# Loading q of the first three attention steps as pairs of tokens in a fused attention and mixture-of-experts kernel

## Chip, cores and metric

One core of one Trainium2 chip runs the whole program. The metric is the device time of one execution, in microseconds (us), as the median of several runs; less is better.

## What is computed

Two blocks follow one another. The first is a lightning attention over q, k and v of shape (4, 8, 768, 64) (batch, heads, tokens, head size), with one decay rate per head. The second is a top-1 mixture of eight experts over the 3072 rows of width 512 that the attention gives. Cut to what matters:

```python
for b in range(S // 64):                     # lightning attention, all of it per batch and head
    intra = (qb @ kb.T * Dmask) @ vb
    inter = (qb * lam_pow) @ kv_state
    out[b] = intra + inter
    kv_state = lam_block * kv_state + (kb * rev_pow).T @ vb
x = out.transpose(0, 2, 1, 3).reshape(3072, 512)
e = argmax(x @ w_gate)                       # one expert per row
y = softmax_max * relu(x @ w1[e]) @ w2[e]
```

## The kernel before

The attention runs in 12 steps of 128 tokens for two batches (`steps`, line 90): step 0 is batches 0 and 1, step 1 batches 2 and 3, both of the first 128 tokens; step 2 is batches 0 and 1 of the next 128 tokens, and so on. A step's q, k and v are one load of 512 KB each (line 117), with a token in a partition and the 16 head rows of 256 bytes beside one another: 2048 packets of 256 bytes. Only step 0 loads its q and k in four parts each (line 115; per half of the heads and per batch, 128 KB). All of these loads are issued by SyncE in the order written, the first nine ahead of the program (lines 124 to 130), later ones by `begin` four steps ahead; they go into three tiles of their own (`q_in`, `k_in`, `v_in`) and two that later hold weights (`room`).

In each step TensorE turns q and k to (head size, tokens): eight products with the identity each into PSUM (`turned`, line 242; `tq` and `tk`), two heads at a time. For each half `s` of the heads, ScalarE copies `tq` to `qT` and `tk` to `kT` (lines 252 and 264). In step 1 alone (`m.n == 0 and m.b > 0`, line 249) VectorE copies `tq` instead. From step 2 on VectorE also multiplies `tq` by `qdec` into `qs_room` (line 256), the query that meets the running state. GpSimd makes `kd` = k times `kdec` (line 270).

Then come, in the order in which TensorE has them: `score` (line 280, `sp`, 32 products; VectorE multiplies by the decay mask into `mt`, line 287, four instructions), the state's part (line 309, from step 2 on), `grow` (line 348, `cp`), `attend` (line 322, `op`), the copy of `op` into `xT` by ScalarE (lines 334 and 340; in step 0 half of the second by VectorE, line 1197), and the gate's products (`lgT`, line 374) and the turn back to rows (`tx`, line 383) in `leave`. TensorE's order is fixed by `pin`, so it waits for whatever its next product needs.

VectorE makes the decay tables once, by scans along tokens: `decay` (line 178, eight scans) and `kdec` (line 183), and then `later_decays` (lines 1010 to 1018): two copies to `lam_pair`, four scans to `qdec`, one copy to `sdec`. Their place is set by `with tc.issue_after(keys_made.ins): later_decays()` (line 1175), right after `kdec`.

After the attention the rows are gathered by expert through lists in memory, and each expert's two products run with weights of 2 MB each.

Of the kernel before, what the change touches and what calls it, by code (L numbers as in the profile page):

```python
# [10 lines left out]
F32 = mybir.dt.float32  # L11
# [12 lines left out]
def kernel(  # L24
# [34 lines left out]
    P = 128  # L59
# [37 lines left out]
    for j, name in enumerate("qkv"):  # L97
        own = [qkv.tile([P, 2, H, D], F32, tag=name, name=f"{name}_in") for i in range(3)]
        homes[name] = own + [
            room[:, j].rearrange("p (b h d) -> p b h d", b=2, h=H) for room in w_room]  # L100

    def load(i, names, first=False):

        if i >= len(steps) or (i, names[0]) in loaded:
            return
        n, b0 = steps[i]
        parts = (slice(0, H // 2), slice(H // 2, H)) if first else (slice(0, H),)
        for name in names:
            loaded[i, name] = homes[name][i % len(homes[name])]
        for hs, name in itertools.product(parts, names):  # L110
            src = {"q": q, "k": k, "v": v}[name][b0:b0 + 2, hs, n * C:(n + 1) * C, :]
            to = loaded[i, name]
            if first:
                for b in range(2):
                    nc.sync.dma_start(out=to[:, b, hs], in_=src[b].rearrange("h s d -> s h d"))
            else:
                nc.sync.dma_start(out=to.rearrange("p b h d -> p (b h) d"),
                                  in_=src.rearrange("b h s d -> s (b h) d"))
# [113 lines left out]
    def pin(inst):  # L232
        tc.keep_in_program_order(inst)
        return inst
# [4 lines left out]
    def turned(src, s, t):  # L239
# [2 lines left out]
            pin(nc.tensor.transpose(t[:, i, b, :], src[:, b, h:h + 2, :], ident))  # L242
        return t

    def turn_q(m, s):
        shp = turned_shape
        tq = turned(m.q, s, bank(2 * s, shp, "tq"))
        qT = work.tile(shp, F32, tag="qT", name="qT")
        if m.n == 0 and m.b > 0:
            pin(nc.vector.tensor_copy(qT, tq))  # L250
        else:
            nc.scalar.copy(qT, tq)
        m.qT.append(qT)
        if m.n > 0:
            qsT = qs_room[:, next(qs_slots)]
            nc.vector.tensor_mul(  # L256
                qsT, tq, qdec[:, s * HP // 2:(s + 1) * HP // 2].unsqueeze(2).to_broadcast(shp))
            m.qsT.append(qsT)
# [913 lines left out]
                mybir.DependencyClass.Sync, mybir.DependencyReason.DATA),  # L1172
                reason="the gathers have the DMA engines first")

    with tc.issue_after(keys_made.ins):
        later_decays()
    idle = bank(5, [P, P], "idle")
    for i in range(10):
        pin(nc.tensor.matmul(idle, lhsT=zeros, rhs=zeros, start=True, stop=True))
# [18 lines left out]
    one = begin(1)  # L1198
    for s in range(2):
        turn_q(one, s)  # L1200
    leave(cur, between=lambda: [turn_k(one, s) for s in range(2)])()
    for s in range(2):
        score(one, s)
# [241 lines left out]
```

## Time and profile before

| | before |
|---|---|
| median of 3 runs | 432.18 us |
| the runs | 431.16, 432.18, 433.41 us |
| the profiled execution's own time | 429.92 us |
| its span, first to last instruction | 428.1 us |
| TensorE busy | 97% of the span |
| VectorE, ScalarE, GpSimd busy | 62%, 41%, 60% |
| TensorE's granted clock | full speed in all 40 slices |

The profile's span is 1.82 us shorter than the time of the same execution, and that execution 2.26 us shorter than the median. All starts below are in us from the start of the span. A chain of waits is followed back from the last instruction: each piece is what released the next. "Issue" pieces and queues such as SPq are time of a sequencer.

### The profile page before, as it was taken

The numbers are of one execution on the slowest core, as the hardware profiler recorded it, in microseconds if no ns is written. First come the engines' busy times: TensorE is split into PE (matmuls) and PEld (weight loads), VectorE is DVE, ScalarE is ACT, GpSimd is POOL, SyncE is SP. The second block draws the span as 40 slices with busy tenths as digits, with TensorE's granted clock in tenths as the row PEclk, the third lists the DMA queues.
The fourth block names the chain that finished last, engine by engine and source line by source line (L and its number), as shares of the span: only waits on it lengthen the run. The fifth ranks groups of instructions, "written<-read, shape, count | busy, mean of one in ns | idle before, by whom it ended". The sixth has DMA issues, their size and how long they took to land.

```text
span 428.1 us, 9730 instructions
## 1 busy us (share of the span) xinstructions
PE 416.5 (97%) x3775; PEld 392.9 (92%) x3776; DVE 265.0 (62%) x587; ACT 174.1 (41%) x319; POOL 255.9 (60%) x209
## 2 busy tenths in 40 slices
PE   8999999999999997999999999999999999999995
PEld 7889999988878986999999999999999999999964
DVE  6656657787566546765558757554775565556454
ACT  3365455565431434350544154345414525331131
POOL 4242657471353357777938856794875878559043
PEclk9999999999999999999999999999999999999999
DMA  9999999999876748968359947966974894652121
GB/s 174 208 240 246 249 240 230 230 233 237 239 257 189 239 63 248 297 190 316 57 123 195 346 81 155 318 183 117 268 276 81 186 380 94 157 200 47 29 78 64
DMA packets 164545, 83.06 MB, mean 194 GB/s; under 512 B 145923, under 2 KB 145959, under 8 KB 164496
## 3 DMA queue, kind: packets, MB, share of 16 engines
q1 hardware_dynamic: 155024, 63.21, 60.9%
q0 software_dynamic: 5536, 12.88, 10.2%
q10 hardware_dynamic: 3936, 6.31, 4.4%
q8 instruction: 31, 0.51, 0.5%
q14 instruction: 18, 0.15, 0.1%
HBM read 58.96 MB, written 12.72 MB: 167 GB/s over the span
## 4 chain that ended last, share of the span: by engine, by line
PE 80%; DVE 5%; DMA 5%; ACT 3%; SPq 2%; POOL 2%; issue 2%; POOLq 0%; ACTq 0%; DVEq 0%
PE p L734 30%; PE p L932 26%; PE sp L280 5%; PE op L322 4%; PE cp L348 2%; PE tk L242 2%; PE tx L383 2%; PE op L309 2%; PE tq L242 2%; PE p L780 2%; DMA xg<-xs,list_0a 1%; PE p L788 1%; DMA xg<-xs,list 1%; PE lgT L374 1%; SPq L583 1%
## 5 line engine op out<-in xcount | busy, mean ns | idle before, releaser
L539 POOL DMA_INDIRECT out_dram<-o_room,list x24 | 25.5, 1064 | 53.9 <-DMA decay<-planes_q 23.0
L745 ACT ACTIVATE hT<-hT 128x418 f32<-128x418 f32 (+6 forms) x56 | 28.1, 520 | 33.1 <-DVE hT L742 32.1
L734 PE MATMUL p<-xgT,w1t 128*128 128x209 f32 (+6 forms) x224 | 41.1, 326 | 0.0
L287 DVE TENSOR_TENSOR mt<-sp,decay 128x512 f32<-128x512 f32 x48 | 29.8, 682 | 14.5 <-PE sp L280 14.4
L734 PEld LDWEIGHTS p<-xgT,w1t 128*128 128x128 f32 x224 | 37.2, 189 | 0.4 <-issue 0.4
L624 ACT COPY u_qT<-p 128x418 f32<-128x418 f32 (+6 forms) x14 | 6.7, 479 | 68.2 <-PE p L734 68.2
L932 PE MATMUL p<-hT,w2t 128*128 128x209 f32 (+5 forms) x192 | 33.6, 328 | 0.0
L472 POOL DMA_INDIRECT slots<-entry,slot_i x24 | 23.8, 990 | 13.8 <-PE tl L397 6.0
L932 PEld LDWEIGHTS p<-hT,w2t 128*128 128x128 f32 x192 | 32.0, 189 | 0.0
L533 POOL DMA_INDIRECT xg<-xs,list x25 | 25.2, 1010 | 11.0 <-issue 6.1
L742 DVE TENSOR_TENSOR hT<-p,u_kd 128x418 f32<-128x418 f32 (+6 forms) x28 | 15.6, 559 | 20.3 <-PE p L734 20.3
L270 POOL TENSOR_TENSOR kd<-k_in,kdec 128x512 f32<-128x512 f32 x12 | 12.4, 1042 | 21.7 <-issue 10.3
L280 PE MATMUL sp<-qT,kT 64*128 64x128 f32 x384 | 24.7, 279 | 0.5 <-DVE qs_room L256 0.5
L661 POOL TENSOR_TENSOR s_q<-w1t 128x1024 f32<-128x1024 f32 x7 | 16.5, 2357 | 14.3 <-DVE t_xT L719 12.6
L280 PEld LDWEIGHTS sp<-qT,kT 64*128 64x128 f32 x384 | 22.5, 188 | 2.6 <-issue 1.7
L734 PE MATMUL p<-st,s_q 128*128 128x209 f32 (+6 forms) x112 | 20.7, 327 | 2.7 <-POOL s_q L661 2.7
L612 PE MATMUL ph<-xgT,w1t 128*128 128x256 f32 (+1 forms) x128 | 21.6, 328 | 0.1
L591 ACT COPY xgT<-decay 128x1672 uint16<-128x1672 uint16 (+6 forms) x7 | 13.6, 1942 | 19.3 <-DMA decay<-planes_k 19.3
L734 PEld LDWEIGHTS p<-st,s_q 128*128 128x128 f32 x112 | 18.6, 190 | 3.0 <-POOL s_q L661 3.0
L612 PEld LDWEIGHTS ph<-xgT,w1t 128*128 128x128 f32 x128 | 19.3, 191 | 1.9 <-DVE xgT L603 0.3
L975 ACT ACTIVATE o_room<-o_room,list 128x512 f32<-128x512 f32 (+6 forms) x22 | 14.1, 710 | 16.5 <-DMA o_room<-qs_room 16.5
L658 POOL TENSOR_TENSOR w1t<-w1t 128x1024 f32<-128x1024 f32 x7 | 20.2, 2893 | 0.6
(260 smaller groups left out, 1092.3 us busy)
## 6 DMA issues: line engine op xcount, KB each, us to landing
w2t<-in_moe_w_dram SPq DMA_DIRECT2D x8, 2048.0 KB, 9.7
w1t<-in_moe_w_dram SPq DMA_DIRECT2D x7, 2048.0 KB, 16.3
xs<-x_room ACTq DMA_DIRECT2D x12, 512.0 KB, 5.8
v_in<-in_v_dram SPq DMA_DIRECT2D x8, 512.0 KB, 9.1
o_room<-qs_room SPq DMA_DIRECT2D x76, 48.0 KB, 2.0
q_in<-in_q_dram SPq DMA_DIRECT2D x7, 512.0 KB, 8.8
k_in<-in_k_dram SPq DMA_DIRECT2D x7, 512.0 KB, 7.5
room<-in_q_dram SPq DMA_DIRECT2D x4, 512.0 KB, 9.0
```

The source lines that it names most:

```text
L242: pin(nc.tensor.transpose(t[:, i, b, :], src[:, b, h:h + 2, :], ident))
L280: m.scored = pin(nc.tensor.matmul(sp[u][:, i, b, :], lhsT=m.kT[s][halves[u], i, b, :], rhs=m.qT[s][halves[u], i, b, :], start=(i == 0 and ...
L287: nc.vector.tensor_mul(mt[:, u], sp[u], decay[:, u, s * HP // 2:(s + 1) * HP // 2].unsqueeze(2).to_broadcast(shp))
L322: pin(nc.tensor.matmul(out_at(m, b, u, hp), lhsT=m.v[:, b, 2 * hp + u, :], rhs=m.mt[hp // 2][:, u, hp % 2, b, :], start=(first and hp == 0 ...
L472: put = nc.gpsimd.indirect_dma_start(out=slots, out_offset=bass.IndirectOffsetOnAxis(ap=slot_i[:, i:i + 1], axis=0), in_=entry[:, n, bs[i] ...
L533: return nc.gpsimd.indirect_dma_start(out=dst, out_offset=None, in_=xs[:rows, :], in_offset=bass.IndirectOffsetOnAxis(ap=idx, axis=0))
L539: put = nc.gpsimd.indirect_dma_start(out=out, out_offset=bass.IndirectOffsetOnAxis(ap=idx, axis=0), in_=src, in_offset=None, bounds_check= ...
L612: nc.tensor.matmul(ph, lhsT=w1t[:, dc, fc * P:(fc + 1) * P], rhs=m.xgT[:, dc, :], start=(dc == 0), stop=(dc == DC - 1))
L658: return nc.gpsimd.tensor_tensor(out=o, in0=x, in1=y, op=ALU.add)
L734: nc.tensor.matmul(p[:, i, :], lhsT=lhs[:, dc, g, i * P:(i + 1) * P], rhs=rhs[:, dc, :], start=(dc == 0), stop=(dc == DH - 1))
L745: pin(nc.scalar.activation(outs[i][k], outs[i][k], ACT.Relu))
L932: nc.tensor.matmul(p[:, c, :], lhsT=lhs[:, f, c * P:(c + 1) * P], rhs=rhs[:, f, :], start=(f == 0), stop=(f == FC // 2 - 1))
```

## The change

It touches q of steps 0, 1 and 2 (`PAIRED = 3`) and the place of `later_decays`.

The load puts two neighbouring tokens of a head into one partition, 512 bytes that lie together in memory: partitions 0 to 63 hold the pairs of one batch, 64 to 127 those of the other, and there is one load for each batch. So q of a step is 1024 packets of 512 bytes instead of 2048 of 256, and steps 1 and 2 have one load more.

TensorE turns such a tile with as many products as before, one head of both batches at a time; in PSUM, even tokens come out in partitions 0 to 63 and odd ones in 64 to 127. To get the old `qT`, four copies of 64 partitions and 256 columns take the place of one of 128 by 512, each written with a step of two columns: ScalarE makes the two for the even heads, VectorE the two for the odd ones. `qs_room` of step 2 is then made from `qT` in SBUF and no longer from `tq` in PSUM.

`later_decays` now comes after the last of VectorE's copies of step 1 (`one.paired`) instead of after `kdec`.

```diff
+    PAIRED = 3
+    def by_pairs(home):
+        return home.rearrange("p b h d -> p (b h d)").rearrange("p (h w) -> p h w", h=H)
...
-            if first:
+            if name == "q" and i < PAIRED:
+                for b in range(2):
+                    nc.sync.dma_start(out=by_pairs(to)[b * D:(b + 1) * D, hs],
+                                      in_=src[b].rearrange("h (t r) d -> t h (r d)", r=2))
+            elif first:
...
+    def turn_pairs(m, s):
+        shp = turned_shape
+        tq = bank(2 * s, [P, HP, 2, D], "tq")
+        for h in range(HP):
+            pin(nc.tensor.transpose(tq[:, h].rearrange("p b t -> p (b t)"),
+                                    by_pairs(m.q)[:, s * HP + h, :], ident))
+        qT = work.tile(shp, F32, tag="qT", name="qT")
+        for u, r in itertools.product(range(2), range(2)):
+            to, of = qT[halves[u], :, :, r::2], tq[halves[r], u::2]
+            if u:
+                m.paired = pin(nc.vector.tensor_copy(to, of))
+            else:
+                nc.scalar.copy(to, of)
+        m.qT.append(qT)
+        if m.n > 0:
+            qsT = qs_room[:, next(qs_slots)]
+            nc.vector.tensor_mul(
+                qsT, qT, qdec[:, s * HP // 2:(s + 1) * HP // 2].unsqueeze(2).to_broadcast(shp))
+            m.qsT.append(qsT)
+
     def turn_q(m, s):
+        if steps.index((m.n, m.b)) < PAIRED:
+            return turn_pairs(m, s)
...
-        if m.n == 0 and m.b > 0:
-            pin(nc.vector.tensor_copy(qT, tq))
-        else:
-            nc.scalar.copy(qT, tq)
+        nc.scalar.copy(qT, tq)
...
-    with tc.issue_after(keys_made.ins):
-        later_decays()
...
     one = begin(1)
     for s in range(2):
         turn_q(one, s)
+    with tc.issue_after(one.paired.ins):
+        later_decays()
```

Three places show what moves on VectorE. The first is step 0, from the scans of `decay` to the first `mt`. Before:

```order
L178 SCALAR_TENSOR_TENSOR decay<-lam_bc,ident 128x128 x8
L1157 COPY ebase_late<-ebase 128x8
L183 COPY kdec<-decay 128x2x4
L1013 COPY lam_pair<-lam_bc 64x4 x2
L1015 SCALAR_TENSOR_TENSOR qdec<-lam_pair,zeros 128x128 x4
L1018 COPY sdec<-qdec 128x4
L287 TENSOR_TENSOR mt<-sp_236,decay 128x512
```

And now:

```order
L188 SCALAR_TENSOR_TENSOR decay<-lam_bc,ident 128x128 x8
L265 COPY qT<-tq 64x256
L193 COPY kdec<-decay 128x2x4
L265 COPY qT<-tq 64x256 x3
L1186 COPY ebase_late<-ebase 128x8
L316 TENSOR_TENSOR mt<-sp_237,decay 128x512
```

The seven instructions of `later_decays` have left step 0, four copies to `qT` have come, and `kdec` stands behind the first of them. The second place is step 1, from the copy of `xT` to the first `mt`. Before:

```order
L1197 COPY xT<-op_267 64x4x128
L250 COPY qT<-tq 128x512 x2
L398 TENSOR_REDUCE lg<-tl 128x16
L287 TENSOR_TENSOR mt<-sp_368,decay 128x512
L287 TENSOR_TENSOR mt<-sp_369,decay 128x512
```

And now:

```order
L1224 COPY xT<-op_268 64x4x128
L265 COPY qT<-tq 64x256 x4
L1042 COPY lam_pair<-lam_bc 64x4 x2
L1044 SCALAR_TENSOR_TENSOR qdec<-lam_pair,zeros 128x128 x4
L427 TENSOR_REDUCE lg<-tl 128x16
L1047 COPY sdec<-qdec 128x4
L316 TENSOR_TENSOR mt<-sp_382,decay 128x512
```

All seven now stand ahead of step 1's `mt`. The third place is step 2, with what each instruction waits for (an engine or a queue of transfers). Before:

```order
L368 COPY st<-cp 128x512 [waits PE_49]
L256 TENSOR_TENSOR qs_room<-tq,qdec 128x512 [waits Activation_49] x2
L287 TENSOR_TENSOR mt<-sp_472,decay 128x512 [waits DVE_49,PE_49]
L287 TENSOR_TENSOR mt<-sp_473,decay 128x512 [waits PE_49]
L287 TENSOR_TENSOR mt<-sp_485,decay 128x512 [waits DVE_49,PE_49]
```

And now:

```order
L397 COPY st<-cp 128x512 [waits PE_49]
L265 COPY qT<-tq 64x256 [waits PE_49,Activation_49]
L265 COPY qT<-tq 64x256
L271 TENSOR_TENSOR qs_room<-qT,qdec 128x512 [waits DVE_49]
L265 COPY qT<-tq 64x256 [waits PE_49,Activation_49]
L265 COPY qT<-tq 64x256
L271 TENSOR_TENSOR qs_room<-qT,qdec 128x512 [waits DVE_49]
L316 TENSOR_TENSOR mt<-sp_492,decay 128x512 [waits PE_49]
```

Two instructions ahead of `mt` have become six, and VectorE's copies wait for ScalarE's of the same `tq`.

## Rows read from the trace of the kernel before

**Rows 1.** The page's table of 40 equal slices (10.7 us each): tenths of busy time of TensorE, and of the 16 DMA engines.

```profile
PE   8999999999999997999999999999999999999995
...
DMA  9999999999876748968359947966974894652121
```

**Rows 2.** The chain of waits of the first 36 us, in order of time: start, length, what.

```profile
4.57 3.61 DMA k_in<-in_k_dram
...
8.78 1.99 PE sp L280 x32
...
13.45 0.59 ACT xT L334
...
14.06 0.59 ACT xT L340
...
14.67 0.69 DVE xT L1197
...
15.51 0.43 PE lgT L374 x8
15.93 1.02 PE tk L242 x8
...
17.94 1.99 PE sp L280 x32
...
21.00 1.55 PE op L322 x28
...
23.77 0.58 ACT xT L340
...
24.38 0.59 ACT qT L252
...
24.99 0.70 DVE qs_room L256
...
25.83 2.14 PE sp L280 x32
```

**Rows 3.** What TensorE waited for between 4 and 30 us: total us, times, longest.

```profile
PE tk L242 <- DMA k_in<-in_k_dram: 0.8, 2, 0.5
PE lgT L374 <- DVE xT L1197: 0.5, 1, 0.5
PE sp L280 <- DVE qs_room L256: 0.5, 1, 0.5
```

**Rows 4.** SyncE's queue in order of time: start, length of the issue, what was issued.

```profile
4.02 1.06 SPq L115 DMA_DIRECT2D k_in<-in_k_dram  x2
5.12 0.51 SPq L117 DMA_DIRECT2D v_in<-in_v_dram  x1
...
7.95 2.33 SPq L117 DMA_DIRECT2D k_in<-in_k_dram  x1
```

**Rows 5.** The list of issues by line, those between 1.2 and 1.8 us: size of one, us from issue to landing.

```profile
q_in<-in_q_dram SPq DMA_DIRECT2D x2, 128.0 KB, 3.3
```

**Rows 6.** Packets that the DMA engines moved in two stretches: from 3 to 15 us (nearly all of 256 bytes), and from 105.9 to 108 us (but for 32 small ones, of 4 KB, the weights).

```profile
DMA packets 10983, 2.66 MB, mean 222 GB/s; under 512 B 10982, under 2 KB 10982, under 8 KB 10982
...
DMA packets 226, 0.80 MB, mean 380 GB/s; under 512 B 32, under 2 KB 32, under 8 KB 226
```

**Rows 7.** VectorE in order of time: start, length, line, operation, count, and idle time before it.

```profile
3.54 2.63 DVE L178 TENSOR_TENSOR_SCAN decay<-lam_bc,ident 128x128 f32<-128x128 f32 x8 [2.25 <-POOL ahead_of L1277]
...
6.29 0.33 DVE L1013 COPY lam_pair<-lam_bc 64x4 f32<-64x4 f32 x2
...
9.61 0.17 DVE L1018 COPY sdec<-qdec 128x4 f32<-128x4 f32 x1
...
17.97 0.22 DVE L398 TENSOR_REDUCE lg<-tl 128x16 f32<-128x64 f32 x1 [1.29 <-PE tl L397]
19.06 2.48 DVE L287 TENSOR_TENSOR mt<-sp,decay 128x512 f32<-128x512 f32 x4 [0.86 <-PE sp L280]
...
27.00 2.48 DVE L287 TENSOR_TENSOR mt<-sp,decay 128x512 f32<-128x512 f32 x4 [0.33 <-PE sp L280]
```

**Rows 8.** Two engines in order of time: the last of VectorE's four scans to `qdec`, and GpSimd's `kd` of step 0 (second half) and of step 1 (both halves).

```profile
8.36 1.22 DVE L1015 TENSOR_TENSOR_SCAN qdec<-lam_pair,zeros 128x128 f32<-128x128 f32 x1
...
8.25 1.04 POOL L270 TENSOR_TENSOR kd<-k_in,kdec 128x512 f32<-128x512 f32 x1 [0.73 <-DMA k_in<-in_k_dram]
...
15.85 2.04 POOL L270 TENSOR_TENSOR kd<-k_in,kdec 128x512 f32<-128x512 f32 x2 [1.66 <-DMA k_in<-in_k_dram]
```

**Rows 9.** Durations of one instruction by line, ns (shortest/median/longest): a ScalarE copy out of PSUM of 128 by 256, a VectorE instruction out of PSUM of 128 by 128, VectorE's copy of `xT` out of PSUM of 64 by 512.

```profile
L386 ACT COPY x_room<-tx x4: 372/382/396, 114.4 to 119.7; 128x256 f32<-128x256 f32 x4
...
L567 DVE TENSOR_SCALAR hT<-ph x8: 290/291/292, 148.8 to 155.1; 128x128 f32<-128x128 f32 x8
...
L1197 DVE COPY xT<-op x1: 684/684/684, 14.7 to 14.7; 64x512 f32<-64x512 f32 x1
```

**Rows 10.** ScalarE in order of time, in step 2: start, length.

```profile
24.86 0.59 ACT L264 COPY kT<-tk 128x512 f32<-128x512 f32 x1
25.33 0.60 ACT L252 COPY qT<-tq 128x512 f32<-128x512 f32 x1
```

**Rows 11.** What SyncE's queue waited for between 36 and 60 us, the longest first: total us, times, longest.

```profile
SPq L117 <- PE sp L280: 6.5, 2, 3.6
```

## The prediction

> **What bounds the kernel now.** I read the page's slices first: TensorE is at nine tenths or more in nearly every one, and so are the DMA engines in the first quarter [rows 1]. A shorter load can pay only where TensorE waits for one, so the next view is what TensorE waits for. From 4 to 30 us its named waits are small: 0.8 us for k, 0.5 for VectorE's half of `xT`, 0.5 for `qs_room` [rows 3]. The chain of waits puts them in order [rows 2]. In step 0 the last part of k, issued at 4.57, lands 3.61 later, at 8.18, and TensorE follows. Step 1 hangs on copies: `xT` by ScalarE at 13.45 and 14.06, by VectorE at 14.67, then the gate's products at 15.51. Step 2 hangs on copies as well: `xT` until 24.35, `qT` at 24.38, `qs_room` at 24.99, and `sp` at 25.83. From there the chain is TensorE alone. So everything that this change can do happens before about 31 us, and what TensorE has gained or lost by then is carried to the end.
>
> No load is on the chain but that of step 0. Later the queue of loads is itself held back: between 36 and 60 us it waits 6.5 us for TensorE to free buffers [rows 11]. A lead that smaller q loads give is lost there.
>
> **Step 0: what the load gives.** The DMA engines move 256-byte packets at 222 GB/s, which is 18.5 ns for a packet on each of 16 engines, and 4-KB packets at 380 GB/s, some 172 ns [rows 6]. No row has 512 bytes. Bounds: the same time per packet (18.5 ns, half the time for the load), or the same GB/s (37 ns, no gain). A line through both rows gives 28.7 ns, nearest to the row of the small packets, and I take it: a 128-KB part of q takes 0.46 us instead of 0.59, and a whole q 1.84 instead of 2.36.
>
> That does not come through in full, because SyncE issues one part each 0.55 us (two k parts in 1.06 us from 4.02, the next at 5.12) [rows 4]. The last k is issued at 4.57 as before. It landed 3.61 us later, and the q parts at the start, with an almost empty queue, 3.3 us after issue [rows 5, 2]. The 0.3 us between is the backlog, and that is all a faster q can remove. **Gain 0.3 us**, between 0 (no faster q) and 0.3.
>
> What step 0 adds is covered. Where ScalarE had one copy to `qT` of 512 columns it has two of 256, at 0.38 us each [rows 9]. Neighbouring ScalarE copies start 0.47 apart though each lasts 0.59 [rows 10], so two of these take 0.65. VectorE's copies of 256 columns lie between its 0.29 (128 columns) and 0.68 (512) [rows 9]; a line between the two gives 0.42, two together 0.76. They end before k, the last to land, is turned and copied. `kdec` slips behind the first of them, by about half a microsecond, and with it the first `kd`; but GpSimd sat idle 0.73 us before the second `kd`, waiting for k [rows 8]. The extra issues of steps 1 and 2 cost SyncE about 0.5 us each [rows 4], in a queue whose issues already take 2.3 us because the engines are full; nobody waits for those q.
>
> **Step 1: the decay tables.** The times here are those of before; the 0.3 us moves all of them alike. VectorE is done with `xT` at 15.36 [rows 2]. ScalarE starts `qT` at 14.66, ends the first pair at 15.3 and the second at 15.9; VectorE's pairs wait for those and end at 16.15 and 16.8. Then come the two `lam_pair` copies (0.33), four scans at 0.33 (eight took 2.63), `lg` (0.22) and `sdec` (0.17) [rows 7]: 16.8 + 0.33 + 1.32 + 0.39 = 18.85. `mt` started at 19.06 [rows 7], so the cover is 0.2 us, and another 0.1 lies behind it: the last `mt` ended at 21.54, and the second half of `op`, which needs it, came at about 21.65 (28 products in 1.55 us from 21.00) [rows 2].
>
> The danger is GpSimd. The last scan took 1.22 us instead of 0.33 beside a `kd`, and ended at 9.58, 0.29 after that `kd` [rows 8]. In step 1 `kd` runs from 15.85 to 17.89 because k lands then. With q of steps 0 and 1 faster, that k lands some 0.8 us sooner (0.3 and 0.52 us), 0.5 more than the rest moves, so `kd` is done at about 17.4 on this scale; the first scan ends at 17.7 instead of 17.5. **Cost 0**, and 0.3 us if q is no faster (first below).
>
> **Step 2: two engines for one `qT`.** ScalarE is free at 24.35 [rows 2]. Before: `qT`, then `qs_room`, done at 25.69, then `sp`. Now ScalarE's pair ends at 25.03, VectorE's pair, which waits for it, at 25.81, and TensorE may start `sp` 0.14 later, as it does now behind `qs_room`: 25.95 instead of 25.83. For the second half of the heads ScalarE is ready at 26.05, but VectorE makes `qs_room` first (0.7, until 26.5) and its pair only until 27.2. TensorE, a microsecond into `sp`, wants it at 26.95 and gets it at 27.35. **Cost 0.5 us.** `mt` starts at 27.9 instead of 27.00 [rows 7] and ends at 30.4, ahead of the next turns into its last bank at about 31. The low bound takes each of VectorE's copies at 0.29 (nothing lost), the high one at 0.68 (below).
>
> **Sum.** -0.3 + 0 + 0.5 = **+0.2 us** on the profiled execution's 429.92, so 430.1. Its median neighbours lie 2.26 higher; on the median of 432.18 the forecast is 432.4.
>
> Here a page speaks against the load's gain. The Trainium skill (SBUF — State Buffer, "Can I just issue two DMAs to hit both halves?") says that a transfer into 64 partitions reaches half of the ports into SBUF, and that two transfers, one for each half, run hardly faster than one. No run here shows it. By its 218 GB/s for 64 partitions, an estimate, q would be no faster than the row's 222 GB/s, and the sum would be that of the first rival.
>
> **The rivals.**
>
> *Half-height loads are no faster.* Each q load now writes 64 partitions instead of 128; if that holds it to the 222 GB/s of [rows 6], step 0 gains nothing, and k of step 1 lands when it did. Then `kd` ends at 17.89, the first scan at 18.18, the other three at 19.17, `mt` starts at about 19.45: 0.4 late, of which 0.1 is covered. With step 2: 0 + 0.3 + 0.5 = +0.8, or 433.0. For it: no row shows a load of half the partitions. Against: 4-KB packets reach 380 GB/s, so at 222 it is the number of packets that sets the time, and that is halved.
>
> *VectorE's copies are slow.* The copies write every second column, for which VectorE has no row. If each of them costs what 512 columns do, 0.68 instead of 0.42, VectorE sets the pace in all three steps. In step 0 its second pair ends at about 10.0 where TensorE wants it at 9.5: +0.6. In step 1 `mt` comes at about 19.85: +0.7. In step 2 the second pair ends at 28.5: +1.7. With the load's 0.3: +2.7, or **434.9, slower than before**. It decides from about 0.6 us for a copy on. For it: one scan of VectorE took over three times its usual time [rows 8], so its durations are not given by size alone. Against: the copies read PSUM, where `xT` took a normal 0.68 although it changes partitions too [rows 9]. The Trainium skill (SBUF — State Buffer, "Door 1: The DMA port swizzle") counts two fp32 values to a 16-byte line as enough for full rate, which is what this step gives; no row here has such a write, and by that rule the rival falls away.
>
> *The copies are cheap.* If a copy of 256 columns takes little over 0.29 us, step 2 costs nothing and only the load's 0.3 remains: 431.9.
>
> **How the numbers follow.** What a measurement of this kernel can tell from no change is about 0.5%, here 2.2 us. Chances: the forecast 0.42, half-height loads 0.27, cheap copies 0.14, slow copies 0.11, and 0.06 for what I have not seen, half of it on either side. The first three lie between 431.9 and 433.0, and runs of one kernel lie up to 1.2 us from their median; so the range is 431.0 to 434.0, and it leaves out the slow copies. TensorE's named waits before 30 us come to 1.8 us [rows 3], less than that even if all went, hence 0.04 for faster; 0.84 for no change; 0.12 for slower.
>
> **What would show it.** Right: the last k of step 0 lands at about 7.9, `sp` of step 0 starts 0.3 earlier, `mt` of step 1 starts without waiting for the scans, the second half of `sp` in step 2 waits for VectorE's `qT`, and TensorE is 0.2 us later from 31 us on. q's loads take about 1.8 us of the queue. Wrong: k of step 0 still lands at 8.2, scans of over 1 us in step 1, copies to `qT` of 0.6 us on VectorE, or any difference that arises after 31 us.

## The result and the profile after

| | before | after |
|---|---|---|
| median, beside each other (9 runs each) | 432.37 us | 434.74 us |
| profiled execution, its span | 429.92, 428.1 us | 433.91, 432.2 us |
| ratio, 95% interval | | 1.0068 [1.0053, 1.0083] |
| again, on another chip (35 and 12 runs) | 430.81 us | 432.99 us, 1.0058 [1.0029, 1.0086] |

By the medians the change makes the kernel 2.2 to 2.4 us slower. The forecast was 432.4, and 434.74 lies beyond its range. One of the 35 runs of before, at 1515.64 us, and one each of before and of experiment 2 at about 1104 us count in the medians below but not in the ratios. In the profile after, L121 issues the parts of q in pairs, L265 and L267 are VectorE's and ScalarE's copies to `qT`, L271 the decay multiply of such a step, L1042 and L1044 the decay tables.

SyncE's queue in order of time, start and length of each issue, answers to [rows 4]:

```profile
0.77 1.42 SPq L121 DMA_DIRECT2D q_in<-in_q_dram  x2
2.24 1.15 SPq L125 DMA_DIRECT2D k_in<-in_k_dram  x2
3.43 1.26 SPq L121 DMA_DIRECT2D q_in<-in_q_dram  x2
4.74 1.16 SPq L125 DMA_DIRECT2D k_in<-in_k_dram  x2
5.94 0.51 SPq L127 DMA_DIRECT2D v_in<-in_v_dram  x1
```

A pair of k parts took 1.06 us before. Here a pair of q parts takes 1.26 to 1.42, and the k parts beside them 1.15. So the last k goes out at 5.39 instead of 4.57, and v at 5.94 instead of 5.12. GpSimd's second `kd` of step 0 waits for that k:

```profile
8.79 1.04 POOL L299 TENSOR_TENSOR kd<-k_in,kdec 128x512 f32<-128x512 f32 x1 [0.38 <-DMA k_in<-in_k_dram]
```

From the issue to this use 3.40 us passed, where it was 3.68 before (4.57 to 8.25, [rows 8]). So k comes 0.28 us sooner behind its issue, and its issue is 0.82 us later.

The packets from 3 to 15 us, the same stretch as in [rows 6]:

```profile
DMA packets 8277, 2.44 MB, mean 204 GB/s; under 512 B 6363, under 2 KB 8277, under 8 KB 8277
```

A quarter fewer packets than the 10983 of before, and fewer bytes too: 204 GB/s against 222. A packet took 17.5 ns before (10983 in 12 us on 16 engines). At that price the 6363 small ones fill 7.0 of the 12 us, and each of the 1914 larger ones would have taken some 42 ns, over twice as much. But this estimate holds only if the engines were as full all the time as before, and while step 0's parts came in they were not. Before and after, from 3 to 8 us (columns: us, busy PE, PEld, DVE, ACT, POOL, clock, DMA share, GB/s; packets overlap, so the share can pass 1):

```profile
3.00:8.00 5.00, 4.55 (x26) 3.45 (x25) 4.41 (x14) 1.52 (x3) 1.66 (x8) 1.00 1.19 231
...
3.00:8.00 5.00, 3.64 (x23) 3.08 (x23) 3.66 (x11) 1.34 (x3) 1.23 (x8) 1.00 1.01 206
```

Over the whole stretch the larger packets moved the bytes no faster; what one of them costs is read below, beside experiment 13.

What TensorE waited for from 4 to 30 us, total, times, longest [rows 3]:

```profile
PE tk L252 <- DMA k_in<-in_k_dram: 1.6, 3, 0.7
PE sp L309 <- DVE qT L265: 1.1, 2, 0.7
PE tq L259 <- DMA q_in<-in_q_dram: 0.6, 1, 0.6
PE lgT L403 <- DVE xT L1224: 0.5, 1, 0.5
PE cp L377 <- DMA v_in<-in_v_dram: 0.2, 1, 0.2
```

Named waits were 2.1 us before (0.3 for q besides those of [rows 3]) and are 4.0 now. VectorE in order of time in steps 1 and 2 [rows 7]:

```profile
16.40 1.76 DVE L265 COPY qT<-tq 64x256 f32<-64x256 f32 x4
18.18 0.99 DVE L1042 COPY lam_pair<-lam_bc 64x4 f32<-64x4 f32 x2
19.20 1.37 DVE L1044 TENSOR_TENSOR_SCAN qdec<-lam_pair,zeros 128x128 f32<-128x128 f32 x4
...
20.82 2.48 DVE L316 TENSOR_TENSOR mt<-sp,decay 128x512 f32<-128x512 f32 x4
...
26.86 0.86 DVE L265 COPY qT<-tq 64x256 f32<-64x256 f32 x2 [2.97 <-ACT qT L267]
27.76 0.69 DVE L271 TENSOR_TENSOR qs_room<-qT,qdec 128x512 f32<-128x512 f32 x1
28.48 0.86 DVE L265 COPY qT<-tq 64x256 f32<-64x256 f32 x2
29.37 1.43 DVE L271 TENSOR_TENSOR qs_room<-qT,qdec 128x512 f32<-128x512 f32 x1
```

And GpSimd beside it [rows 8]:

```profile
16.93 2.04 POOL L299 TENSOR_TENSOR kd<-k_in,kdec 128x512 f32<-128x512 f32 x2 [1.69 <-PE lgT L403]
...
29.19 1.05 POOL L389 TENSOR_TENSOR sd<-st,sdec 128x512 f32<-128x512 f32 x1
```

Four copies of 0.42 us take 1.76: they run one behind the other, with no overlap. The two `lam_pair` copies take 0.99 instead of 0.33 and end just behind `kd` (18.97). `mt` starts 2.00 us after its `sp` (18.82); before it was 1.19 (17.87 to 19.06). The second multiply takes 1.43 and ends 0.56 after `sd`.

TensorE before, at `cp` of step 0, the first turns of step 2 and the state products of step 3:

```profile
10.73 1.15 PE L348 MATMUL cp<-v_in,kd 128*64 128x64 f32 x32
...
22.68 0.66 PE L242 MATMUL tq<-ident,q_in 128*128 128x128 f32 x4
...
31.35 1.10 PE L309 MATMUL op<-qs_room,st 64*64 64x128 f32 x32
```

And after, with all of step 2's scores:

```profile
11.65 1.15 PE L377 MATMUL cp<-v_in,kd 128*64 128x64 f32 x32 [0.18 <-DMA v_in<-in_v_dram]
...
24.37 0.66 PE L259 MATMUL tq<-ident,q_in 128*128 128x128 f32 x4
...
27.87 1.16 PE L309 MATMUL sp<-qT,kT 64*128 64x128 f32 x16 [0.65 <-DVE qT L265]
29.49 1.16 PE L309 MATMUL sp<-qT,kT 64*128 64x128 f32 x16 [0.45 <-DVE qT L265]
30.58 0.64 PE L403 MATMUL lgT<-xT,gates 128*32 128x128 f32 x16
...
34.03 1.10 PE L338 MATMUL op<-qs_room,st 64*64 64x128 f32 x32
```

So TensorE is 2.68 us late at the state products: 0.92 from step 0 (`cp` at 11.65 instead of 10.73), 0.77 from step 1 (the turns of step 2 begin 1.69 late), 0.99 from step 2.

### The profile page after: what moved, and what is told of

Its sections match the earlier page's. It is cut to its first block, busy times and chain, and to the rows that moved or that the text cites. A ratio compares the mean times of both kernels' runs of the same rounds, so it can differ in the third digit from the quotient of the medians.

```text
span 432.2 us, 9757 instructions
## 1 busy us (share of the span) xinstructions
PE 418.9 (97%) x3775; PEld 394.1 (91%) x3776; DVE 267.8 (62%) x597; ACT 176.6 (41%) x327; POOL 255.9 (59%) x209
## 4 chain that ended last, share of the span: by engine, by line
PE 86%; DVE 6%; ACT 2%; issue 2%; DMA 1%; SPq 1%; POOL 0%; ACTq 0%; POOLq 0%; DVEq 0%
PE p L763 29%; PE p L961 26%; PE ph L641 5%; PE p L809 4%; PE op L351 4%; PE sp L309 4%; PE tx L412 2%; PE op L338 2%; PE cp L377 2%; PE tq L252 2%; PE tk L252 2%; DMA v_in<-in_v_dram 1%; PE p L817 1%; PE lgT L403 1%; ACT xT L369 1%
## 5 line engine op out<-in xcount | busy, mean ns | idle before, releaser
L774 ACT ACTIVATE hT<-hT 128x418 f32<-128x418 f32 (+6 forms) x56 | 27.9, 520 | 32.3 <-DVE hT L771 28.7
L562 POOL DMA_INDIRECT xg<-xs,list x25 | 26.1, 1043 | 8.2 <-issue 6.3
L763 PE MATMUL p<-t_sd,w1t 128*128 128x209 f32 (+6 forms) x112 | 20.7, 327 | 0.1
L363 ACT COPY xT<-op 128x512 f32<-128x512 f32 x12 | 7.0, 585 | 33.3 <-PE op L351 19.7
```

Source lines behind the costliest of these rows:

```text
L562: return nc.gpsimd.indirect_dma_start(out=dst, out_offset=None, in_=xs[:rows, :], in_offset=bass.IndirectOffsetOnAxis(ap=idx, axis=0))
L763: nc.tensor.matmul(p[:, i, :], lhsT=lhs[:, dc, g, i * P:(i + 1) * P], rhs=rhs[:, dc, :], start=(dc == 0), stop=(dc == DH - 1))
L774: pin(nc.scalar.activation(outs[i][k], outs[i][k], ACT.Relu))
```

## The experiments

Each row has the starts, in us, of TensorE's groups in one profiled execution: scores (`sp`) of steps 0, 1 and 2, `cp` of step 0, the state products of step 3 and how far behind before's they are, and the ratio of the timed runs to those of before on the same chip. Medians of before differ from chip to chip (429.99 to 432.37), so only ratios compare. Experiments 1 to 4 shared one chip, and so did 5 to 8, 9 to 12 and 13 to 16.

| kernel | sp 0 | cp 0 | sp 1 | sp 2 | state 3 | late | ratio [95%] |
|---|---|---|---|---|---|---|---|
| before | 8.71 | 10.73 | 17.87 | 25.83 | 31.35 | | |
| after | 9.24 | 11.65 | 18.82 | 27.87 | 34.03 | 2.68 | 1.0068 [1.0053, 1.0083] |
| e1 step 0 only | 10.59 | 12.57 | 19.72 | 27.68 | 33.21 | 1.86 | 1.0061 [1.0040, 1.0083] |
| e2 step 1 only | 8.70 | 11.21 | 18.35 | 26.31 | 31.83 | 0.48 | 1.0021 [0.9999, 1.0042] |
| e3 step 2 only | 8.68 | 10.69 | 17.83 | 26.16 | 32.77 | 1.42 | 1.0020 [1.0007, 1.0034] |
| e4 scans only | 8.77 | 10.79 | 17.93 | 26.32 | 31.84 | 0.49 | 0.9999 [0.9984, 1.0015] |
| e5 step 0 and scans | 9.36 | 11.86 | 19.00 | 27.37 | 32.89 | 1.54 | 0.9989 [0.9956, 1.0022] |
| e6 q 0 from ScalarE | 11.29 | 15.01 | 22.16 | 30.57 | 38.19 | 6.84 | 1.0090 [1.0052, 1.0127] |
| e7 before, q 0 from ScalarE | 9.60 | 11.58 | 18.72 | 26.69 | 32.21 | 0.86 | 1.0033 [0.9998, 1.0068] |
| e8 multiplies late | 8.73 | 11.45 | 18.59 | 27.52 | 33.34 | 1.99 | 1.0037 [1.0005, 1.0069] |
| e9 before again | 8.57 | 10.72 | 17.86 | 25.82 | 31.34 | -0.01 | 1.0003 [0.9968, 1.0039] |
| e10 after again | 9.00 | 11.83 | 18.97 | 27.79 | 37.71 | 6.36 | 1.0058 [1.0029, 1.0086] |
| e11 half height | 11.23 | 13.21 | 20.36 | 28.32 | 33.85 | 2.50 | 1.0070 [1.0035, 1.0105] |
| e12 steps 1 and 2 | 8.69 | 11.16 | 18.37 | 27.43 | 33.60 | 2.25 | 1.0045 [1.0016, 1.0074] |
| e13 two issues | 9.77 | 12.64 | 19.79 | 28.86 | 35.35 | 4.00 | 1.0085 [1.0052, 1.0117] |
| e14 two issues, step 0 | 9.48 | 11.68 | 18.92 | 27.19 | 32.71 | 1.36 | 1.0023 [0.9997, 1.0049] |
| e15 two issues, late | 10.21 | 12.77 | 20.01 | 29.07 | 34.90 | 3.55 | 1.0059 [1.0027, 1.0091] |
| e16 before, two issues | 9.96 | 12.61 | 19.76 | 27.73 | 33.25 | 1.90 | 1.0037 [1.0012, 1.0062] |

### One part at a time

In e1 to e3 one step alone is paired and the scans stay where they were; e4 pairs nothing and moves the scans.

```
-    PAIRED = 3
+    PAIRED = (0,)
...
-            if name == "q" and i < PAIRED:
+            if name == "q" and i in PAIRED:
...
+    with tc.issue_after(keys_made.ins):
+        later_decays()
...
-    with tc.issue_after(one.paired.ins):
-        later_decays()
```

That is e1, cut; a step that is not paired has its q copied as before the change. `PAIRED` is `(1,)` in e2, `(2,)` in e3, and empty in e4, which keeps the scans' new place, as do e5 with `(0,)` and e12 with `(1, 2)`.

> Only step 0's q is loaded in pairs and put back by halves; steps 1 and 2 and the place of the four scans are as before. Theory (SyncE's issues): a 64-partition part with 512-byte packets holds SyncE 0.61 to 0.76 us where the part before held it 0.50, so the last k part is issued at about 5.4 instead of 4.57 us, TensorE's first sp starts at about 9.2 instead of 8.71, and the kernel is 0.5 to 0.9 us slower (432.9 to 433.3). Rival (issues don't matter, the path is hidden behind VectorE's first scans and GpSimd's kd): sp late but cp at 10.7 as before, 432.2 to 432.5. Rival (the half-height loads land later, not the issues): issue to landing grows beyond 3.4 us.

Slower by as much as the whole change, but for a reason that I had not foreseen in this form: VectorE's copies of step 0 stood behind the four scans, and TensorE waited 1.60 us for them.

> Only step 1's q is loaded in pairs; the four scans stay where they were before, ahead of it. Theory (step 1 lost because of the scans' new place, not because of the copies): VectorE's four 64x256 copies of 0.43 us take the place of two of 0.68 us, mt of step 1 starts within 0.3 us of 19.06 us, total 432.2 to 432.7. Rival (the copies cost): mt of step 1 0.8 us late, total 433.0 to 433.4.

The expected size, from another place. Step 1 itself is covered, but `cp` of step 0 waited 0.5 us:

```profile
PE cp L380 <- DMA v_in<-in_v_dram: 0.5, 1, 0.5
```

Nothing before v differs from before here. What differs is the q that is issued right behind v. TensorE waits for v at `cp` in after, e2, e8, e10, e12 and e13, all with step 1 in pairs, and not in e3, e4 and e7. But it waits 0.2 us in e5 too, where v was only issued late, and not in e6 and e15, which have step 1 in pairs and come to `cp` later; so the paired q behind it is a likely cause and not a shown one.

> Only step 2's q is loaded in pairs. Theory (VectorE's chain copy, copy, multiply stands ahead of mt, and scores wait for the second half's copies): sp of step 2 0.3 us late, lgT 0.9 us late (28.8 instead of 27.90), total 433.0 to 433.4. Rival (the +0.9 us in step 2 is a follow-on of the delays of steps 0 and 1): lgT within 0.3 us of 27.90, total 432.2 to 432.7.

Step 2 costs more alone (1.42) than its share of the whole (0.99). VectorE in order of time:

```profile
25.15 0.86 DVE L265 COPY qT<-tq 64x256 f32<-64x256 f32 x2 [3.04 <-ACT qT L267]
26.05 1.09 DVE L271 TENSOR_TENSOR qs_room<-qT,qdec 128x512 f32<-128x512 f32 x1
27.17 0.86 DVE L265 COPY qT<-tq 64x256 f32<-64x256 f32 x2
28.06 1.55 DVE L271 TENSOR_TENSOR qs_room<-qT,qdec 128x512 f32<-128x512 f32 x1
```

GpSimd's `kd` ran until 26.59 and its `sd` from 28.00 to 29.05, so both multiplies end about 0.55 after it. In the kernel before the first of them took 0.69 in the middle of a `kd` (24.99 to 25.68, `kd` from 23.87 to 25.91). It read `tq` in PSUM there; now both operands lie in SBUF.

That `kd` meets the first multiply at all is the load's doing:

```profile
24.52 0.63 PE L252 MATMUL tk<-ident,k_in 128*128 128x128 f32 x4 [1.22 <-DMA k_in<-in_k_dram]
```

Before, this turn began at 23.85 after a wait of 0.51 us. The two loads of step 2's q held SyncE for 4.49 us where the one took 3.79, k behind them went out 0.66 later (17.34 for 16.68) and came 0.67 later, and with it `kd`. At the old time `kd` would have been done by 25.91, ahead of the multiply at 26.05. (In the whole change this k went out at 18.41; there `kd` was done at 27.78, and the first multiply, from 27.76 on, took 0.69.)

> All loads and copies as before; only the four scans with their two small copies are moved behind VectorE's copies of step 1. Theory (the scans' new place costs step 1): the lam copies wait for GpSimd's kd (about 1 us in all instead of 0.33), mt of step 1 starts 0.5 to 0.9 us late, total 432.8 to 433.4. Rival (VectorE has the room there): mt within 0.2 us of 19.06, total 432.2 to 432.6. Rival (a delay only arises after 40 us, from the phase of the engines): the parts of these four runs don't add up to the 2.4 us of the whole change.

The place was right and the total was not. `lam_pair` took 1.32 us beside `kd`, as VectorE's rows show:

```profile
16.66 1.32 DVE L1045 COPY lam_pair<-lam_bc 64x4 f32<-64x4 f32 x2
...
19.63 2.47 DVE L319 TENSOR_TENSOR mt<-sp,decay 128x512 f32<-128x512 f32 x4
```

`mt` came 0.57 late and the state products 0.49, but the runs show no loss; the interval's upper end is 0.65 us. The four parts add to 4.25 us at the state products (e1 to e4) and the whole to 2.68. Half of the difference is that in e1 VectorE's copies stand behind the scans, which moving them removes (e5 less e4, below, is 1.05 instead of 1.86); the rest is overlap of the waits.

### Step 0: issues, or bytes

> Step 0's q in pairs, and the four scans moved behind VectorE's copies of step 1 as in the whole change; steps 1 and 2 load q as before. With step 0 alone and the scans left in place the kernel lost 2.3 us, since VectorE's copies of step 0 then stood behind the scans (sp at 10.59 us). Theory (the copies' place behind the scans was most of that; what is left is SyncE's longer issues): sp of step 0 starts at 8.8 to 9.3 us, cp at 10.8 to 11.7, total 0.4 to 1.0 us over before. Rival (the pairs cost step 0 as much with the scans out of the way): 2 us over before or more.

`sp` and `cp` start 0.06 and 0.16 us behind the theory's ranges, and the state products 1.05 us later than with the scans alone. The total misses: no loss at all, though the interval reaches 0.95 us.

In e6 and e7 the four q parts of step 0 go out from ScalarE's queue:

```
-                    nc.sync.dma_start(out=by_pairs(to)[b * D:(b + 1) * D, hs],
+                    (nc.scalar if first else nc.sync).dma_start(out=by_pairs(to)[b * D:(b + 1) * D, hs],
```

```
-                    nc.sync.dma_start(out=to[:, b, hs], in_=src[b].rearrange("h s d -> s h d"))
+                    (nc.scalar if name == "q" else nc.sync).dma_start(
+                        out=to[:, b, hs], in_=src[b].rearrange("h s d -> s h d"))
```

> The whole change, but the four q parts of step 0 are issued from ScalarE's queue, beside SyncE's k parts instead of between them. Theory (what step 0 loses is time in which SyncE issues): the last k part is issued at about 3 us instead of 5.39, sp of step 0 starts at 8.3 us or before instead of 9.24, total 0.7 to 1.2 us less than the whole change, 1.2 to 1.8 over before. Rival (the transfers themselves are the limit in the first 8 us): sp within 0.3 us of 9.24, total as the whole change, 2.2 to 2.6 over before.

> The kernel before, with step 0's four q parts issued from ScalarE's queue. Theory (issues are the limit before too): sp of step 0 starts 0.4 to 1 us before 8.71, total 0.3 to 0.8 us less than before. Rival (VectorE's scans, which end at 9.8 us, or the transfers hold step 0): mt still starts at 9.9, total within 0.2 us of before.

Both misses. In e6 ScalarE's issues are as long as SyncE's were (shortest, median, longest, in ns), the fourth comes after a pause and is out at 4.43, and TensorE saw its first q at 7.53, because q landed late:

```profile
L121 ACTq DMA_DIRECT2D q_in<-in_q_dram x4: 602/633/693, 1.3 to 3.8; - x4
...
DMA to landing us min/median/max: 5.4/5.9/6.3
```

All four k parts were out by 2.90 and in flight beside q. In e7 q landed 3.7 to 5.6 us after issue, and TensorE waited 1.1 us for it before its scores, at unchanged packets. Two queues side by side did not bring q sooner: with the issues out of each other's way the transfers took longer, as e6's rival has it, though `sp` lies far outside the rival's range too (the clock stood at 0.52 from 8 to 12 us).

In e11 the parts have the shape of the change, 64 partitions, with the packets of before:

```
+            if first and name == "q":
+                ts = slice(2 * D * hs.start // H, 2 * D * hs.stop // H)
+                for b in range(2):
+                    nc.sync.dma_start(out=to[ts, b], in_=q[b0 + b, :, ts, :].rearrange("h s d -> s h d"))
```

> The kernel before, with each 128 KB q part of step 0 cut by tokens instead of heads: 64 partitions, 8 heads, 256-byte packets, so 512 packets as before, in place of 128 partitions and 4 heads; the first turn of q then waits for all four parts. Theory (SyncE's time for an issue goes with the half-height shape, not with the number of packets): each of these issues takes 0.6 us or more. Rival (it is the 512-byte packets or the paired view): 0.50 us as before. sp of step 0 is 0.3 to 1 us late either way, total 432.4 to 433.4 beside a before of 432.

The issues are those of the whole change almost to the nanosecond. The list for q of its issues (shortest, median, longest, in ns):

```profile
L116 SPq DMA_DIRECT2D q_in<-in_q_dram x4: 607/629/755, 0.8 to 4.1; - x4
...
DMA to landing us min/median/max: 3.6/3.8/3.9
```

In the whole change they are 607, 614 and 756. So the shape sets SyncE's time for an issue, and packets of 512 bytes instead of 256 change nothing in it. Landing takes 3.8 us after issue, where the full-height parts took 3.3 [rows 5] to 3.5. The last k, issued at 5.45, was used 3.60 us later. (TensorE's scores are much later here because the first turn needs all four parts.) The stretch from 3 to 8 us, columns as above:

```profile
3.00:8.00 5.00, 2.29 (x14) 1.92 (x13) 4.41 (x14) 0.00 (x0) 1.65 (x8) 0.94 1.17 197
```

With q in half height and packets of 256 bytes the engines, as full as before (1.17 for 1.19), moved 197 GB/s instead of 231; with packets of 512 bytes they moved 206 at a share of 1.01. So half the partitions cost something, and the larger packets gave it back per busy time, as far as one profile of each tells.

In e13 to e16 step 0's q comes in two issues of 256 KB (here as in e13 to e15; e16 does it to the kernel before, over 128 partitions):

```
+                if hs.start:
+                    continue
+                whole = q[b0:b0 + 2, :, n * C:(n + 1) * C, :]
                 for b in range(2):
-                    nc.sync.dma_start(out=by_pairs(to)[b * D:(b + 1) * D, hs],
-                                      in_=src[b].rearrange("h (t r) d -> t h (r d)", r=2))
+                    nc.sync.dma_start(out=by_pairs(to)[b * D:(b + 1) * D],
+                                      in_=whole[b].rearrange("h (t r) d -> t h (r d)", r=2))
```

> The whole change, but step 0's q comes in two issues of 256 KB (64 partitions, 8 heads, 512-byte packets) in place of four of 128 KB. Theory (step 0 loses by the four longer issues of SyncE that stand ahead of the last k part): that part is issued at about 4.2 us instead of 5.39, sp of step 0 starts 0.4 to 0.8 us before the 9.0 to 9.24 us of the whole change, the state products of step 3 by as much before theirs (34.0 us), the total 0.4 to 1 us less than the whole change (1.5 to 2 over before). Rival (bytes, not issues, hold the first 8 us): the last k part lands when it did, sp at 9.0 to 9.3.

> Only step 0 by pairs, in two issues of 256 KB, with the scans moved behind VectorE's copies of step 1. Theory: sp of step 0 at 8.4 to 8.9 us, the state products of step 3 0.5 to 1.0 us after those of before (the scans' place alone cost 0.49 there), total 0 to 0.6 us over before. Rival (v, issued behind, then lands late): cp still at 11.5 us or later, state products 1.2 us or more late.

> The kernel before, with step 0's q in two issues of 256 KB over 128 partitions (256-byte packets) in place of four of 128 KB. Theory (issues of SyncE set when step 0's last k lands): the last k part is issued 0.5 us or more before 4.57 us and sp of step 0 starts 0.2 to 0.5 us before 8.71, total 0 to 0.4 us less than before. Rival (bytes hold it): sp within 0.15 us of 8.71 or later.

All three against the theory. In e13 the last k was indeed issued sooner, at 4.00 (the four k parts went out from 2.24 to 4.93), but TensorE's first turn of q came at 7.05 instead of 5.18, and its `sp` at 9.77. That turn now needs all of q, 512 KB, and no longer half of it; so none of the three tests the issues alone. In e16 SyncE's time went up where the number went down:

```profile
1.90 3.69 SPq L118 DMA_DIRECT2D k_in<-in_k_dram  x4
...
L118 SPq DMA_DIRECT2D k_in<-in_k_dram x4: 507/508/2045, 1.9 to 5.1; - x4
```

Four k parts took 2.11 us in two pairs in before and 3.69 here: the first of them, behind the two larger parts of q, took 2.05, the other three 0.51 as ever. (In e16 the clock was at 0.50 for part of step 0, which makes its `sp` later still; in e13 and e14 it was 1.00 all through.) So issues are no fixed price: they differ with their shape and with their place in the queue. How much of step 0's loss is issue time and how much the transfers these four runs do not separate.

What a packet costs they do show. From 3 to 4 us nearly all packets in flight are q's of 512 bytes in e13, and q's and k's of 256 bytes in before (packets, MB, share of 16 engines, for SyncE's queue; e13 first):

```profile
q1 hardware_dynamic: 472, 0.24, 89.4%
...
q1 hardware_dynamic: 1024, 0.26, 113.3%
```

That is 30 ns for a packet of 512 bytes into 64 partitions and 18 ns for one of 256 into 128.

### Step 2, and the parts together

In e8 the two multiplies of step 2 come behind its `mt` products:

```
-            nc.vector.tensor_mul(
+            m.decayed.append(lambda: pin(nc.vector.tensor_mul(
...
     for s in range(2):
         score(ahead, s)
+    with tc.issue_after(ahead.mt_made.ins):
+        for decay_q in ahead.decayed:
+            decay_q()
```

> The whole change, but VectorE's two decay multiplies of step 2 come after its four mt products instead of after each half's copies. Theory (in step 2 the second half's copies wait for the first multiply, and mt for the second, which took 1.43 us beside GpSimd): sp's second half starts without a wait and mt 1.5 us earlier, lgT at about 29.5 instead of 30.58, total 0.7 to 1.1 us less than the whole change. Rival (the multiplies are only displaced: the state products of step 3 wait for them, or the copies alone hold TensorE): the state products still start 2.4 us or more after those of before (31.35), total as the whole change.

Between theory and rival: 0.69 us less at the state products, a ratio of 1.0037 for 1.0068 or 1.0058 on other chips, with intervals that overlap. VectorE in order of time:

```profile
28.68 2.57 DVE L316 TENSOR_TENSOR mt<-sp,decay 128x512 f32<-128x512 f32 x4
31.17 1.28 DVE L271 TENSOR_TENSOR qs_room<-qT,qdec 128x512 f32<-128x512 f32 x2
```

Away from GpSimd's work the two multiplies take 1.28 together, where they took 0.69 and 1.43, and nobody waits for them. But not all of the 0.69 is the edit's: the turns of step 2, ahead of it, already begin 0.36 us sooner than in after (24.01 for 24.37), since step 0 happened to run sooner. That leaves 0.33 us in step 2.

> The whole change with both mends: step 0's q in two issues, and VectorE's two decay multiplies of step 2 behind its mt products. Theory (the mends add up): the state products of step 3 1.0 to 1.6 us after those of before instead of 2.7, total 0.7 to 1.5 us over before. Rival (what one mend gives back the next wait takes): 1.9 us late there or more.

The mends don't add up, since the first is none: 3.55 us late against the 4.00 of e13. From the turns of step 2 on (25.58 and 25.36) the late multiplies are worth 0.67 here.

> The whole change without step 0: steps 1 and 2 load q in pairs, the scans are behind VectorE's copies of step 1. Theory (each step brings its own part of the loss): the state products of step 3 start 1.6 to 2.1 us after those of before (step 0's 0.6 to 1.0 us are gone), the median 1 to 1.8 us over before. Rival (step 0 makes the loss and the others are hidden behind it): 0.5 us or less.

About as expected in the runs (1.45 us over before by the medians, 1.9 by the ratio); at the state products 2.25, above the range. Step 0 adds 0.43 to that, less than the 1.05 that it costs alone (e5 less e4): the waits overlap. The timed runs say the same: steps 1 and 2 with the scans bring most of the loss, and step 0 with the scans (e5) shows none.

### The same chip, and the clock

> The kernel before, unchanged, profiled and timed beside the changed one on the same chip. The profiles so far fall in two kinds after 74 us: in some (before, e5 to e8) the eighth step's lgT to the next step's op takes 3.6 us and TensorE waits for nothing, in others (the changed kernel, e1 to e4) it takes 4.2 us and TensorE waits 0.8 us for ScalarE's xT near 97 to 99 us. Theory (that is a matter of the chip or the execution, not of the change): this profile and that of the changed kernel beside it are of one kind, and the ratio of this kernel to before is 1.000 within 0.3%. Rival (the change makes the late loss of 1.7 us): this one is of the first kind, the changed one of the second.

> The whole change, unchanged, beside the kernel before on the same chip. Theory (the loss is made before 34 us, 0.9 us in step 0, 0.8 in step 1, 0.9 in step 2): the state products of step 3 start 2.4 to 2.9 us after those of before, and the median is 1.9 to 2.9 us over it. Rival (most of it arises after 34 us): 1 us or less over before at the state products, or a median that is over 3.5 us higher.

Theory in e9: the late loss of 1.7 us, which the first pair of profiles showed between 74 and 118 us, is not tied to the change. Both profiles of this chip, of the kernel before and of the changed one, are of the first kind, with 3.6 us at that place. In e10 the median is as expected, but not the state products, 6.36 late. TensorE's granted clock tells it (columns: us, busy PE, PEld, DVE, ACT, POOL, clock, DMA share, GB/s):

```profile
28.00:30.20 2.20, 0.95 (x16) 0.77 (x15) 2.12 (x4) 0.61 (x2) 2.07 (x3) 0.89 0.99 279
30.20:36.00 5.80, 5.79 (x45) 5.16 (x46) 3.17 (x5) 1.44 (x3) 0.00 (x0) 0.50 1.13 259
```

TensorE, in order of time:

```profile
27.79 1.16 PE L309 MATMUL sp<-qT,kT 64*128 64x128 f32 x16 [0.95 <-DVE qT L265]
30.21 2.08 PE L309 MATMUL sp<-qT,kT 64*128 64x128 f32 x16 [1.27 <-DVE qT L265]
32.22 1.08 PE L403 MATMUL lgT<-xT,gates 128*32 128x128 f32 x16
```

A first multiply of 1.50 us made TensorE wait 1.27 us more, it had worked 0.95 of 2.2 us, and the clock went from 2.4 to 1.2 GHz for some 6 us: the same 16 products took 2.08 instead of 1.16. From `lgT` to the state products passed 5.49 us instead of 3.45. So a gap that VectorE makes can cost twice. It need not: in e13 TensorE waited 1.44 and 0.79 us at the same two places, and the clock stayed at 1.00. In e6, e11, e15 and e16, where TensorE waited for q at the start, products of step 0 ran at 0.50 for a microsecond or more as well. The runs fit: of the 34 of before on this chip 16 had a mean granted clock of 0.997 or more, median 429.17, of the 12 of the whole change two, at 431.91 and 432.26; the others have medians of 431.45 and 433.65. That the change lowers the clock more often is thus possible and not shown; of its first nine runs five were at 0.997 or more. Why this multiply took 1.50, with `kd` done at 27.40, is open: GpSimd was issuing two transfers until 28.80 and began `sd` then, but in the first profile of the same kernel the first multiply took 0.69 beside the same issues.

Nor does a delay at 31 us come through whole. In e9 TensorE waits for the gather of tokens ahead of the first expert layer, and in e10, 3.3 us later, it doesn't:

```profile
121.30 0.98 PE L598 MATMUL tp<-ident,xg 128*128 128x128 f32 x7 [1.05 <-DMA xg<-xs,list_0a]
```

```profile
124.62 1.04 PE L627 MATMUL tp<-ident,xg 128*128 128x128 f32 x8
```

In e5, 1.54 late at the state products, this layer's first products start at 121.20, against 121.10 in before. How much of a delay survives there differs from execution to execution, and that I have not settled; it is the likeliest reason why e4 and e5 show no loss in the runs.

## Why the prediction was wrong

The sum was -0.3 + 0 + 0.5; the profile has 0.92 + 0.77 + 0.99 at the state products. Each step cost more than its term, for the most part through something that had been put at nothing.

- **What bounds the kernel.** Right that what the change does is done by the state products: 2.68 us late there, and e10 shows that the rest of the first pair's difference is not tied to the change. Wrong that all of it is carried to the end.
- **Step 0, "SyncE issues one part each 0.55 us", "the last k is issued at 4.57 as before": the first step that failed.** The half-height shape alone takes 0.61 to 0.76 (e11), and k was issued 0.82 late. The time of an issue was taken from another shape. q's second half was turned at 7.83 instead of 7.06, and `sp` started 0.53 later and took 2.23 instead of 2.06. Behind it v came late too, which I had not priced. Step 0 cost 0.92 at `cp` instead of giving 0.3. That issues were the whole of it is not shown: e6, e13 and e16 changed them and lost, for reasons of their own.
- **Step 0, the load's gain (-0.3): about right, and outweighed.** From its issue to GpSimd's use the last k took 0.28 us less than before, where the backlog had been priced at 0.3 (0.60 in e1, 0.16 in e5; 0.08 in e11, with small packets and the same issues). The price of 28.7 ns for a packet of 512 bytes, "a line through both rows", is near the 30 ns of e13. The Trainium skill (SBUF — State Buffer, "Can I just issue two DMAs to hit both halves?") lets two transfers, one to each half, gain 6% over one. The trace does not bear out the 218 GB/s that I had set beside it: in e13 q's two halves moved 239 GB/s from 3 to 4 us. That half height costs something at equal packets e11 shows (197 for 231 GB/s).
- **Step 1, cost 0 or 0.3: mis-sized.** VectorE's copies took 0.42 as estimated, but "start 0.47 apart though each lasts 0.59" does not carry over to these: ScalarE's pair took 0.77 to 0.80 instead of 0.65, VectorE's 0.86 instead of 0.76. The scans were not what GpSimd held up; the small `lam_pair` copies ahead of them were, 0.99 for 0.33. I had `kd` end sooner because q would; it ended 1.1 us later. Measured 0.77 in the whole, 0.49 for the scans' place alone (e4).
- **Step 2, cost 0.5: the order right, the size off.** Copy, multiply, copy stands as I put it, and the second half waits for it. I gave the multiply the 0.7 of before although its operand moved from PSUM to SBUF. Where it met GpSimd it took 1.09 to 1.55. The Trainium skill (SBUF — State Buffer, "Who interferes with whom") has it: a VectorE instruction with two SBUF inputs contends with a GpSimd one that reads SBUF, and it doesn't with one input from PSUM. The trace agrees, in e3 twice and in after and e12 once each, ending 0.55 to 0.57 us after GpSimd's. In e10 and e13 one multiply (1.50 and 1.02 us) began ahead of GpSimd's `sd` and ended in the middle of it, and `sd` took 1.27 us instead of 1.05. Moving both multiplies away from GpSimd's work gave back 0.33 (e8) to 0.67 us (e15). And "nobody waits for those q" left out the k behind them: alone, the extra load of step 2 brought it 0.67 us later (e3).
- **The rivals.** "Half-height loads are no faster" had too low a price, 0.8 (its `mt` adds up to 19.56 and not 19.45, 0.1 more): it kept the issues, v and the multiplies at nothing. "VectorE's copies are slow" came nearest in time, 434.9, by luck: it is false, 418 to 431 ns each.
- **What held.** VectorE's copies cost what the estimate said, the second half of `sp` in step 2 waits for them, nobody gains from faster q, and faster had a chance of 0.04 (from named waits of 1.8 us that are 2.1). The range was too narrow because issues, v, the small copies and the k behind the extra load were each taken to cost nothing.

## What to carry to other kernels

Larger packets need not pay when the load loses half its partitions and gets longer issues for it: price a DMA's issue by its own shape, and ask what is queued behind it. When a change moves an operand from PSUM to SBUF, the same VectorE instruction has a new neighbour in GpSimd; look at what GpSimd does in that microsecond before giving it the old duration. A profile of one execution decides a place and the timed runs on one chip a total, and the two can differ by a microsecond.

## What the runs showed of the hardware

- SyncE's time for a 128-KB issue was 0.50 us over 128 partitions and 0.61 to 0.76 over 64, with packets of 256 or 512 bytes alike (e11); ScalarE's was 0.60 to 0.69 over 64 (e6). One k part behind two parts of 256 KB took 2.05 us, the next three 0.51 (e16).
- With few others in flight a packet of 512 bytes into 64 partitions took 30 ns (e13), one of 256 bytes into 128 partitions 18 (before).
- At the same packet size and share of busy DMA engines, q parts over 64 partitions brought 197 GB/s where parts over 128 brought 231 (e11 and before, 3 to 8 us).
- A VectorE multiply of 128 by 512 with both operands in SBUF ended 0.55 us after the GpSimd instruction that it had met (1.09, 1.43 and 1.55 us instead of 0.69). Two copies of 64 by 4 with both ends in SBUF took 0.99 and 1.32 us instead of 0.33 and ended up to 0.2 us behind GpSimd's `kd`.
- After waits of 0.95 and 1.27 us with 16 products between them TensorE's granted clock was 0.50 (1.2 GHz) for about 6 us (e10); after waits of 1.44 and 0.79 us at the same places it stayed at 1.00 (e13).
